# Three row transposes moved into the end of attention, the others moved behind the selection's spreading products, its scan and its ranks

## The chip, the cores and the metric

The kernel runs on one core of a Trainium2 chip. The metric is the device time of one execution in microseconds (us); the median of several executions is compared. The profile shows one execution, taken by the hardware profiler. Its engines are PE (TensorE matrix products; PEld are its weight loads), DVE (VectorE), ACT (ScalarE), POOL (GpSimd) and SP (which here only issues DMAs).

## The reference

Local attention with a few global keys, then a mixture of experts that keeps at most 80 tokens an expert:

```python
# attention: B=4, H=8, S=768, D=64; keep = 8 global keys, or the last 96 keys
scores = q @ k.T / sqrt(D) - slope[h] * dist          # masked where not kept
x = softmax(scores) @ v                               # 3072 rows of 512
# experts: E=8, F=1024
logits = x @ w_gate
expert_idx, gate_w = argmax(logits), max(softmax(logits))
for e in range(E):
    tok_idx = rows with expert_idx == e, the 80 with the largest gate_w
    out[tok_idx] = gate_w * (relu(x[tok_idx] @ w1[e]) @ w2[e])   # all other rows are 0
```

## The kernel before

The 3072 rows are 24 tiles of 128. The work has three parts one behind the other. **Attention** takes half a tile a step, 48 steps in all: scores, exponential, transposes, product with the values. Its result stays in SBUF turned: `uts[t]` holds tile t with the 512 features on the partitions. The gate's logits are computed on the way. The steps left at the end are written out by hand in the string `DRAIN`, one letter group for each call; the last idle products there are `busy(..., 4)`.

**Selection** (`slots`, `select`) finds the 80 best rows of each expert by a search in five rounds. A round's first product is the spreading product `jb` (L487): it hands a count of the round before (`gs`) to all partitions. DVE then rescales the keys (L489), takes a maximum (L495) and compares in three pieces (L502); PE counts the comparisons with 24 small products `cnt` (L507), and DVE compares the counts with the capacity (L511, `gs`). That is one chain between PE and DVE, each waiting for the other. The fifth round has no comparison: after L489 come two masks (L515, L516), a scan on DVE (L520), three products `rk` that turn the scan into ranks (L519, L522, L523), two DVE steps that make `slot` of them, four comparisons `at` (L556), 24 products `ix` (L560) and the reduction to row numbers `gi` (L563).

Beside this chain the 24 tiles are turned back and written to DRAM as rows, for the gathers: `rows(t, ...)` is four PE transposes into a PSUM tile `xp` (three buffers), one ACT copy (L97) into one of six places in SBUF (`room`, slot t % 6) and one DMA of 256 KB on SP's queue (L98). `slots` is a generator, and at each of its `yield`s `select` puts in `ROWS[i]` such tiles and `WARM[i]` idle products (`busy`, 480 columns, read by nobody). `SPLIT` says at which yield ACT rounds three weight pieces (`early`, L550). There are nine yields: after each round's maximum, after each round's `gs`, and after the ranks. All four compute engines run in the order in which the code is written. A copy into `room` waits until the DMA of the tile six before it has landed.

**Experts**: POOL gathers the rows of each expert from DRAM (L589), which needs `gi` and all 24 row DMAs; PE turns them (L621) and then computes the two layers (L627) without a pause to the end, while weights stream in.

PSUM has eight banks. Attention's pool `psa` uses seven, tags `sc` (two buffers of two banks), `tp0`, `tp1` and `u`. Selection opens its pools over the same banks.

Of the kernel before, what the change touches and what calls it, by code (L numbers as in the profile page):

```python
# [10 lines left out]
F32 = mybir.dt.float32  # L11
# [10 lines left out]
E, DM, DF = 8, 512, 1024  # L22
P = 128
NB = S // P
NT = B * NB
TURN = [*range(NT - NB), *range(NT - NB + 1, NT), NT - NB]
NP = H // 2
# [21 lines left out]

DRAIN = (  # L50
    "r a1 t45 w44 r r r n47 r r a2 t46 r r r r w45 r r r "
    "t47 w46 r b1 w47 r r b2 c1 c c2 c r r c3 r r c c r"
)
NORM = (("V", slice(2, 4)), ("G", slice(0, 2)))
ROWS = (4, 2, 5, 2, 4, 1, 3, 3, 0)
WARM = (0, 0, 0, 0, 1, 0, 0, 0, 9, 5)
SPLIT = (7, 8, 8)
FAR = 1.0e6
END = object()
SLOPES = [2.0 ** -(h + 1) for h in range(H)]  # L60
# [2 lines left out]
def fast_path(tc, a, out, cst, x_dram, inp):  # L63
    nc = tc.nc
# [3 lines left out]
    with ExitStack() as ctx:  # L68
# [20 lines left out]
                    in_=cst["zero"].unsqueeze(1).broadcast_to([P, 2, DM]),  # L89
                )  # L90

        def rows(t, pool, x):
            ut = uts.pop(t)
            xp = pool.tile([P, NP, P], F32, tag="xp", name=f"xp{t}")
            for pr in range(NP):
                T.transpose(out=xp[:, pr, :], in_=ut[:, pr, :], identity=ident)  # L96
            A.copy(out=x, in_=xp.rearrange("p q k -> p (q k)"))  # L97
            nc.sync.dma_start(out=x_dram[TURN[t] * P:(TURN[t] + 1) * P, :], in_=x)  # L98

        with tc.tile_pool(name="at_sb", bufs=2) as sp, tc.tile_pool(name="ps_a", bufs=1, space=PSUM) as psa, ExitStack() as pctx:  # L100
# [160 lines left out]
            def collect(t):  # L261
                g = next(i for i in range(len(GROUPS)) if t < sum(GROUPS[:i + 1]))
                n, t0 = GROUPS[g], sum(GROUPS[:g])
                if t == t0:
                    st["rt"] = Route(nc, sp, cst, t0, n)
                rt = st["rt"]
                if n < 3:
                    rt.one(lgs(t), t - t0)
                else:
                    lp = part(t).rearrange("p (q k) -> p k q", q=NP)  # L270
                    V.tensor_reduce(out=rt.lg[:, t - t0, :], in_=lp[:, :E, :], axis=AX.X, op=ALU.add)
                    if t == t0 + n - 1:
                        routing.append(rt.all())
                if t == t0 + n - 1:
                    if t < NT - 1:
                        routing.append(rt.rest(lps[:, 3 * P:3 * P + E], cst["capm"]))
# [5 lines left out]
            def go(g, n):  # L282
                for _ in islice(g, n):
                    pass

            def routes(n):
                for _ in range(n):
                    while routing and next(routing[0], END) is END:
                        routing.pop(0)
# [9 lines left out]
            for u in range(nu - 1):  # L299
# [47 lines left out]
                w44=lambda: weigh(u - 3), w45=lambda: weigh(u - 2), w46=lambda: weigh(u - 1), w47=lambda: weigh(u),  # L347
                n47=lambda: norm(u), a1=lambda: logits1(NT - 4, 2), a2=lambda: logits2(NT - 4, 2), b1=lambda: logits1(NT - 2, 1),
                b2=lambda: logits2(NT - 2, 1), c1=lambda: logits(NT - 1, (0, 1)), c2=lambda: logits(NT - 1, (2, 3)),
                c3=lambda: collect(NT - 1), r=lambda: routes(1), c=lambda: go(choice, 1),  # L350
            )
            for k in DRAIN.split():
                step[k]()
                if k == "b2":
                    rt = st["rt"]
                    choice, end = rt.choose(), rt.finish()
            scratch = psa.tile([P, 2, 512], F32, tag="sc", bufs=2, name="scratch")
            busy(nc, cst, scratch[:, 0], 4)
            go(choice, 99)
            routes(99)  # L360
            assert not routing
# [5 lines left out]

        hip = pool(name="hi", bufs=NHI[0], side="right")
        early = [hip.tile([P, DF], F32R, tag="hi", name=f"early{i}") for i in range(3)]
        room = inp.kt[1].rearrange("p q k -> p (q k)")[:, :6 * DM].rearrange("p (n d) -> p n d", n=6)  # L370
        select(tc, cst, lps, gs1, rows, raw, early, room)
        rctx.close()
        for _ in chain(wipe, ahead):
            pass
# [101 lines left out]
def slots(nc, sp, s2, pp, cst, gs, cap, slot):  # L476

    V, T, re, oh = nc.vector, nc.tensor, cst["re"], cst["oh"]
    k = P
    for i in range(5):
        n = 15 if i == 3 else 31
        jb = pp.tile([P, E], F32, tag="jb", name=f"jb{i}")
        T.matmul(jb, cst["ones32" if n > 15 else "ones16"][:k, :], gs[:k], start=True, stop=True)  # L487

        V.scalar_tensor_tensor(  # L489
            out=re, in0=re, scalar=512.0 if i == 0 else n + 1.0, in1=jb.unsqueeze(1).broadcast_to([P, NT, E]), op0=ALU.mult, op1=ALU.subtract,  # L490
        )
        if i == 4:
            break
        r = cst["left"][:, i % 2]
        V.tensor_reduce(out=r, in_=re, axis=AX.X, op=ALU.max)  # L495
        yield 1
        cm = s2.tile([P, NT, n], BF16, tag=f"cm{n}", name=f"cm{i}")
        cn = pp.tile([n, E], F32, tag="cnt", name=f"cnt{i}")
        t0 = 0
        for m in CUTS:  # L500
            tq = slice(t0, t0 + m)
            V.tensor_tensor(  # L502
                out=cm[:, tq, :], in0=r[:, tq].unsqueeze(2).broadcast_to([P, m, n]),
                in1=cst["kval"][:, :n].unsqueeze(1).broadcast_to([P, m, n]), op=ALU.is_ge,
            )
            for t in range(t0, t0 + m):
                T.matmul(cn, cm[:, t, :], oh[:, t, :], start=t == 0, stop=t == NT - 1)  # L507
            t0 += m
        k = n
        gs = s2.tile([k, E], BF16, tag=f"gs{n}", name=f"gs{i}")  # L510
        V.tensor_tensor(out=gs, in0=cn, in1=cap[:k], op=ALU.is_ge)  # L511
        yield 1
    mz = cst["mz"].rearrange("p (k t) -> p k t", k=2 * E)
    rev = re.rearrange("p t e -> p e t")
    V.tensor_scalar(out=mz[:, :E, 1:], in0=rev, scalar1=0.0, scalar2=None, op0=ALU.is_gt)  # L515
    V.tensor_scalar(out=mz[:, E:, 1:], in0=rev, scalar1=0.0, scalar2=None, op0=ALU.is_equal)  # L516
    cum = sp.tile([P, 2 * E, NT + 1], BF16, name="cum")
    rk = pp.tile([P, 2 * E, NT], F32, tag="rk", name="rk")
    T.matmul(rk, cst["tri"], mz[:, :, 1:], start=True, stop=False, skip_group_check=True)  # L519
    V.tensor_tensor_scan(  # L520
        out=cum.rearrange("p k t -> p (k t)"), data0=cst["keep"], data1=cst["mz"], initial=0.0, op0=ALU.mult, op1=ALU.add)
    T.matmul(rk[:, E:, :], cst["ones"], cum[:, :E, NT:NT + 1].broadcast_to([P, E, NT]), start=False, stop=False, skip_group_check=True)  # L522
    T.matmul(rk, cst["ones"], cum[:, :, :NT], start=False, stop=True, skip_group_check=True)  # L523
    yield 1
    wk = sp.tile([P, 2 * E, NT], F32, name="wk")
    V.tensor_tensor(out=wk, in0=rk, in1=mz[:, :, 1:], op=ALU.mult)
    with nc.allow_low_precision(reason="a sum of one integer and zeros; where slot is bfloat16, those up to 256 alone are asked for"):
        V.tensor_reduce(out=slot, in_=wk.rearrange("p k t -> p t k"), axis=AX.X, op=ALU.add)


def select(tc, cst, lps, gs1, rows, w, early, room):

    nc = tc.nc
    V, G, T = nc.vector, nc.gpsimd, nc.tensor
# [2 lines left out]
    with tc.tile_pool(name="sel2", bufs=2) as s2, tc.tile_pool(name="ps_s", bufs=1, space=PSUM) as pp, \  # L537
            tc.tile_pool(name="ps_r", bufs=3, space=PSUM) as pr, tc.manual_schedule(engines=ORDERED):
        slot = s2.tile([P, NT], BF16, name="slot", bufs=1)
        late = iter(range(NT))  # L540

        def more(n):
            for t in islice(late, n):
                rows(t, pr, room[:, t % 6])

        for i, _ in enumerate(slots(nc, s2, s2, pp, cst, gs1, cst["cap8"], slot)):
            more(ROWS[i])
# [605 lines left out]
```

## Time and profile before

| | |
|---|---|
| median of 3 runs | 287.97 us (286.52 to 288.28) |
| the profiled execution | 289.09 us, of which the span of its instructions is 287.4 us |
| PE busy in the span | 256.0 us (89%) |
| DVE, ACT, POOL busy | 215.0, 209.7, 123.2 us |
| bytes moved by DMA | 73.06 MB |

The profiled execution is 1.12 us above the median, and 1.7 us of it lie outside the span. Busy shares are means over the three parts, and the change touches the 30 us between 152 and 182 us of the span.

### The profile page before, as it was taken

How to read it: one execution, taken by the hardware profiler on the slowest of the kernel's cores; microseconds unless marked ns; L12 is line 12 of the kernel's file. 1: busy time of each engine (PE TensorE's matmuls, PEld its weight loads, DVE VectorE, ACT ScalarE, POOL GpSimd, SP SyncE). 2: the span in 40 equal slices, each digit the busy share in tenths (PEclk: the TensorE clock that was granted, in tenths of full speed). 3: DMA queues.
4: the chain of work that ended last, by engine and by line, in shares of the span. 5: the costliest groups of instructions: out<-in, count | busy, mean ns of one | idle time of the engine just before them, and what ended most of it. 6: DMA issues, size and time to landing. Idle time of an engine off the chain costs nothing. (4 is left out here: it accounts for less than half of the span.)

```text
span 287.4 us, 9517 instructions
## 1 busy us (share of the span) xinstructions
PE 256.0 (89%) x3538; PEld 187.0 (65%) x3538; DVE 215.0 (75%) x790; ACT 209.7 (73%) x596; POOL 123.2 (43%) x171
## 2 busy tenths in 40 slices
PE   2698799998988999999989997999999999999991
PEld 1486667676665777786757884466566666666660
DVE  4967567886657987689875346789998898988940
ACT  2778669976777968987863775378787978879730
POOL 5365554543553536553454000781506236063351
PEclk9999999999999999999996899799999999999998
DMA  6999999999999983541000794599999989990001
GB/s 180 326 339 378 291 368 323 316 339 320 349 379 392 383 269 115 141 137 42 2 5 20 294 381 187 148 294 348 395 386 395 397 320 401 336 375 16 25 15 41
DMA packets 37674, 73.06 MB, mean 254 GB/s; under 512 B 3284, under 2 KB 10324, under 8 KB 37620
## 3 DMA queue, kind: packets, MB, share of 16 engines
q1 hardware_dynamic: 36452, 69.74, 70.9%
q0 software_dynamic: 1024, 2.62, 3.0%
q8 instruction: 30, 0.49, 0.7%
q14 instruction: 24, 0.20, 0.2%
q10 hardware_dynamic: 144, 0.00, 0.0%
HBM read 58.46 MB, written 13.89 MB: 252 GB/s over the span
## 5 line engine op out<-in xcount | busy, mean ns | idle before, releaser
L145 ACT ACTIVATE pwz<-ts,nm 128x168 f32<-128x168 f32 (+1 forms) x192 | 80.1, 419 | 33.1 <-DVE nm L141 31.8
L158 POOL TENSOR_TENSOR pwz<-pwz,z 128x672 f32<-128x672 f32 (+2 forms) x48 | 60.2, 1253 | 71.4 <-ACT pwz L145 50.0
L141 DVE CUSTOM_DVE_ANT_0 ts<-sc,tab 128x168 f32<-128x168 f32 (+1 forms) x192 | 53.0, 314 | 27.0 <-PE sc L132 27.0
L132 PE MATMUL sc<-kt,q 64*64 64x104 f32 (+3 forms) x1088 | 44.4, 282 | 10.9 <-DVE kt L921 5.3
L608 POOL TENSOR_TENSOR w_3l<-w,w_3h 128x1024 fp32r<-128x1024 f32 x8 | 23.3, 2918 | 51.4 <-issue 34.6
L132 PEld LDWEIGHTS sc<-kt,q 64*64 64x64 f32 x1088 | 34.4, 141 | 14.4 <-issue 13.0
L145 ACT ACTIVATION_READ_ACCUMULATOR pwz<-ts,nm 128x1 f32 x192 | 36.0, 187 | 0.0
L203 PE MATMUL u<-ta,va 104*64 104x128 f32 (+1 forms) x384 | 32.5, 291 | 0.3 <-ACT kt L228 0.3
L174 PE MATMUL tp<-ident,pwz 64*128 64x64 f32 x384 | 22.9, 239 | 9.1 <-ACT ta L184 5.3
L608 DVE TENSOR_TENSOR w_0l<-w,w_0h 128x1024 fp32r<-128x1024 f32 x15 | 25.3, 1689 | 6.1 <-ACT w_0h L605 6.1
L174 PEld LDWEIGHTS tp<-ident,pwz 64*128 64x128 f32 x384 | 16.9, 142 | 17.3 <-POOL pwz L158 9.9
L213 PE MATMUL u<-ta,vb 64*64 64x64 f32 x640 | 27.3, 224 | 0.0
L213 PEld LDWEIGHTS u<-ta,vb 64*64 64x64 f32 x640 | 21.8, 134 | 6.9 <-issue 5.8
L185 DVE COPY ta<-tp 128x384 f32<-128x384 f32 (+1 forms) x48 | 25.4, 529 | 0.5 <-PE tp L174 0.3
L203 PEld LDWEIGHTS u<-ta,va 104*64 104x64 f32 (+1 forms) x384 | 20.6, 139 | 7.3 <-issue 3.1
L184 ACT COPY ta<-tp 128x384 f32<-128x384 f32 (+1 forms) x48 | 21.1, 440 | 1.4 <-PE tp L174 1.4
L608 DVE TENSOR_TENSOR w_2l<-w,w_2h 128x1024 fp32r<-128x1024 f32 x15 | 19.8, 1318 | 0.0
L97 ACT COPY kt<-xp 128x512 f32<-128x512 f32 x24 | 13.6, 589 | 6.9 <-PE xp L96 5.6
L608 DVE TENSOR_TENSOR w_1l<-w,w_1h 128x1024 fp32r<-128x1024 f32 x15 | 18.2, 1211 | 0.0
L605 ACT CAST w_2h<-w 128x1024 fp32r<-128x1024 f32 x15 | 15.9, 1057 | 1.2 <-PE hp L627 1.2
L605 ACT CAST w_3h<-w 128x1024 fp32r<-128x1024 f32 x16 | 16.7, 1044 | 0.0
L141 DVE DVE_READ_ACCUMULATOR2_ANT nm<- 128x1 f32 x192 | 15.8, 82 | 0.0
(391 smaller groups left out, 536.5 us busy)
## 6 DMA issues: line engine op xcount, KB each, us to landing
w<-in_w_dram SPq DMA_DIRECT2D x64, 512.0 KB
out_dram<-zero SPq DMA_DIRECT2D x12, 512.0 KB
x_dram<-kt SPq DMA_DIRECT2D x24, 256.0 KB
q<-in_q_dram SPq DMA_DIRECT2D x23, 256.0 KB
vb<-in_vb_dram SPq DMA_DIRECT2D x20, 256.0 KB
va<-in_va_dram SPq DMA_DIRECT2D x20, 208.0 KB
kt<-in_kT_dram SPq DMA_DIRECT2D x4, 816.0 KB
kt<-in_kT_dram SPq DMA_DIRECT2D x3, 544.0 KB
```

The costliest lines, as they stand in the source:

```text
L97: A.copy(out=x, in_=xp.rearrange("p q k -> p (q k)"))
L132: T.matmul(sc[64 * i:64 * i + 64, hh, pp, o:o + e - c], q[h, pr * P + 64 * i:pr * P + 64 * i + 64], kt[h, pr, c0 + c:c0 + e], start=True, ...
L141: V.tensor_tensor_reduce(out=ts[:, j, :w], in0=sc[:, hh, pp, :w], in1=cst["tab" if m else "tab0"][:, 2 * g + pp, hh, :], scale=-0.125, sca ...
L145: A.activation(out=pw[:, j, :w], in_=ts[:, j, :w], func=AF.Exp, bias=nm[:, j:j + 1], scale=-1.0, accum_out=z[:, j:j + 1],)
L158: eng.tensor_tensor(out=p, in0=p, in1=zs.unsqueeze(2).broadcast_to(list(p.shape)), op=ALU.mult)
L174: T.transpose(out=tps[i][:, 64 * j:64 * j + 64], in_=pw[hs[i], o:o + P], identity=ident[hs[i], hs[i]])
L184: A.copy(out=ta[:, 0, :n], in_=tps[0][:, :n])
L185: V.tensor_copy(out=ta[:, 1, :n], in_=tps[1][:, :n])
L203: T.matmul(up[64 * hh:64 * hh + 64, pr, :], va[:n, 64 * h:64 * h + 64], ta[:n, :, 64 * j:64 * j + 64], start=pp == 0 and (g == 0 or last), ...
L213: T.matmul(up[h, pr, 64 * i:64 * i + 64], vb[h, i, pr, :], ta[h, i, 256 + 64 * pp:320 + 64 * pp], start=False, stop=True, skip_group_check ...
L605: A.copy(out=hi, in_=src)
L608: eng.tensor_tensor(out=lo, in0=src, in1=hi, op=ALU.subtract)
```

## The change

`rows` is cut in two: `turned` issues the four transposes, `stored` the copy and the DMA. One iterator `due` hands the tiles out in order.

- In `DRAIN` the letters `x x x` turn tiles 0 to 2 ahead of `c3`, into PSUM tiles of attention's pool (tags `tp1`, `u`, `sc`), and `y y y` copy and store them behind `c3`. The four idle products go.
- In `slots` the yield after each `gs` goes; in its place are one in the fifth round behind L489 and one behind the scan. Seven yields are left: after each of the first four rounds' maximum, after the fifth round's L489, after the scan, after the ranks.
- `ROWS`, `WARM` and `SPLIT` become (4, 3, 3, 3, 2, 2, 4), three idle products after the ranks and five after `ix`, and the roundings of weights all behind the ranks.

```diff
 DRAIN = (
     "r a1 t45 w44 r r r n47 r r a2 t46 r r r r w45 r r r "
-    "t47 w46 r b1 w47 r r b2 c1 c c2 c r r c3 r r c c r"
+    "t47 w46 r b1 w47 r r b2 c1 c c2 c r r x x x c3 y y y r r c c r"
 )
-ROWS = (4, 2, 5, 2, 4, 1, 3, 3, 0)
-WARM = (0, 0, 0, 0, 1, 0, 0, 0, 9, 5)
-SPLIT = (7, 8, 8)
+ROWS = (4, 3, 3, 3, 2, 2, 4)
+WARM = (0, 0, 0, 0, 0, 0, 3, 5)
+SPLIT = (6, 6, 6)
...
-        def rows(t, pool, x):
+        room = inp.kt[1].rearrange("p q k -> p (q k)")[:, :6 * DM].rearrange("p (n d) -> p n d", n=6)
+        due = iter(range(NT))
+
+        def turned(t, xp):
             ut = uts.pop(t)
-            xp = pool.tile([P, NP, P], F32, tag="xp", name=f"xp{t}")
             for pr in range(NP):
-                T.transpose(out=xp[:, pr, :], in_=ut[:, pr, :], identity=ident)
-            A.copy(out=x, in_=xp.rearrange("p q k -> p (q k)"))
+                T.transpose(out=xp[:, pr * P:pr * P + P], in_=ut[:, pr, :], identity=ident)
+            return t, xp
+
+        def stored(t, xp):
+            x = room[:, t % 6]
+            A.copy(out=x, in_=xp)
             nc.sync.dma_start(out=x_dram[TURN[t] * P:(TURN[t] + 1) * P, :], in_=x)
...
-                c3=lambda: collect(NT - 1), r=lambda: routes(1), c=lambda: go(choice, 1),
+                c3=lambda: collect(NT - 1), x=lambda: edge.append(turned(next(due), spare.pop(0)())), y=lambda: stored(*edge.pop(0)), r=lambda: routes(1), c=lambda: go(choice, 1),
             )
+            edge = []
+            spare = [
+                lambda: psa.tile([P, 512], F32, tag="tp1", name="xp0"), lambda: psa.tile([P, 512], F32, tag="u", name="xp1"),
+                lambda: psa.tile([P, 2, 512], F32, tag="sc", bufs=2, name="xp2")[:, 0],
+            ]
...
-            scratch = psa.tile([P, 2, 512], F32, tag="sc", bufs=2, name="scratch")
-            busy(nc, cst, scratch[:, 0], 4)
...
@@ slots
         if i == 4:
+            yield 1
             break
...
         V.tensor_tensor(out=gs, in0=cn, in1=cap[:k], op=ALU.is_ge)
-        yield 1
...
     V.tensor_tensor_scan(
         out=cum.rearrange("p k t -> p (k t)"), data0=cst["keep"], data1=cst["mz"], initial=0.0, op0=ALU.mult, op1=ALU.add)
+    yield 1
...
@@ select
-            for t in islice(late, n):
-                rows(t, pr, room[:, t % 6])
+            for t in islice(due, n):
+                rows[1](*rows[0](t, pr.tile([P, DM], F32, tag="xp", name=f"xp{t}")))
```

The order of instructions on DVE, ACT, POOL and SP stays; only PE's changes. At the end of attention PE's rows stood so before (`lps<-oh,cf` are the counts of the last groups of tiles, `scratch` the idle products, `jb` the first spreading product):

```order
L473 LDWEIGHTS cf_3213
L473 MATMUL lps<-oh,cf_3213 127x8
L466 LDWEIGHTS ones
L466 MATMUL scratch<-svx,ones 128x480
L473 LDWEIGHTS cf_3260
L473 MATMUL lps<-oh,cf_3260 127x8
L487 LDWEIGHTS ones_75
L487 MATMUL jb_3329<-gs_82,ones_75 128x8
L96 MATMUL xp_3333<-ident,ut_379 128x128 x4
```

The two `ones`/`scratch` rows stand there four times; shown once. Now:

```order
L481 LDWEIGHTS cf_3213
L481 MATMUL lps<-oh,cf_3213 127x8
L98 MATMUL xp_3269<-ident,ut_379 128x128 x4
L98 MATMUL xp_3274<-ident,ut_379 128x128 x4
L98 MATMUL xp_3279<-ident,ut_630 128x128 x4
L481 LDWEIGHTS cf_3260
L481 MATMUL lps<-oh,cf_3260 127x8
L495 LDWEIGHTS ones_75
L495 MATMUL jb_3345<-gs_82,ones_75 128x8
```

Twelve transposes stand where four idle products stood. The `jb` behind them is the first instruction on a bank of selection's pools. In the built program it waits for ACT's last read of attention's PSUM: before, that was the exponential in `c3` (L397); now it is the third of the copies `y`.

From the fourth round to the fifth, PE's rows stood so before (the last `cnt` of the fourth round first):

```order
L507 MATMUL cnt_3587<-oh,cm_3586 15x8
L96 MATMUL xp_3617<-ident,kt_103 128x128 x4
L96 MATMUL xp_3624<-ident,kt_103 128x128 x4
L96 MATMUL xp_3631<-ident,kt_103 128x128 x4
L487 LDWEIGHTS ones_75
L487 MATMUL jb_3639<-gs_3637,ones_75 128x8
L519 LDWEIGHTS tri
L519 MATMUL rk<-mz,tri 128x384
L522 MATMUL rk<-cum,ones 128x192
L523 MATMUL rk<-cum,ones 128x384
L466 LDWEIGHTS ones
L466 MATMUL lps<-svx,ones 128x480
```

The last two stand there nine times. Now:

```order
L495 MATMUL jb_3576<-gs_3574,ones_75 128x8
L98 MATMUL xp_3579<-ident,ut_2403 128x128 x4
L98 MATMUL xp_3586<-ident,ut_2403 128x128 x4
L527 MATMUL rk<-mz,tri 128x384
L98 MATMUL xp_3599<-ident,kt_103 128x128 x4
L98 MATMUL xp_3606<-ident,kt_103 128x128 x4
L531 MATMUL rk<-cum,ones 128x192
L532 MATMUL rk<-cum,ones 128x384
L98 MATMUL xp_3615<-ident,kt_103 128x128 x4
L98 MATMUL xp_3622<-ident,kt_103 128x128 x4
L98 MATMUL xp_3629<-ident,kt_103 128x128 x4
L98 MATMUL xp_3636<-ident,kt_103 128x128 x4
```

The three tiles between the last `cnt` and `jb` are gone, and eight tiles now stand behind `jb`: two ahead of `rk`, two inside it and four behind, followed by three idle products. In the rounds before, nothing stands between `cnt` and the next `jb` any longer either.

## Rows read from the trace of the kernel before

**Rows 1.** The page: the span in 40 slices of 7.2 us, PE's granted clock in tenths of full speed, and GB/s moved.

```profile
PEclk9999999999999999999996899799999999999998
GB/s 180 326 339 378 291 368 323 316 339 320 349 379 392 383 269 115 141 137 42 2 5 20 294 381 187 148 294 348 395 386 395 397 320 401 336 375 16 25 15 41
```

**Rows 2.** Stretches of the span: start and end, length, then busy us (count) of PE, PEld, DVE, ACT and POOL, PE's granted clock (1.00 is 2.4 GHz, 0.50 is 1.2 GHz), DMA share and GB/s.

```profile
152.50:153.00 0.50, 0.49 (x6) 0.45 (x6) 0.32 (x3) 0.14 (x1) 0.00 (x0) 0.69 0.00 0
...
159.00:159.50 0.50, 0.50 (x19) 0.48 (x17) 0.00 (x0) 0.37 (x1) 0.00 (x0) 0.50 0.73 262
159.50:160.00 0.50, 0.50 (x5) 0.50 (x6) 0.15 (x1) 0.00 (x0) 0.00 (x0) 0.98 1.05 393
...
160.00:165.00 5.00, 5.00 (x60) 4.29 (x59) 1.98 (x7) 4.27 (x9) 0.00 (x0) 1.00 0.76 279
165.00:170.00 5.00, 5.00 (x64) 4.23 (x64) 3.26 (x11) 4.03 (x8) 0.00 (x0) 1.00 1.02 381
...
180.00:180.50 0.50, 0.50 (x3) 0.15 (x1) 0.41 (x4) 0.00 (x0) 0.00 (x0) 0.50 0.00 0
183.00:183.50 0.50, 0.50 (x3) 0.21 (x2) 0.50 (x1) 0.00 (x0) 0.24 (x1) 0.59 0.49 94
```

**Rows 3.** The timeline at the end of attention and in the first round: start us, length us, engine, line, operation, result <- operands, shape, count, and in brackets the idle time before it and what ended that.

```profile
152.60 0.44 PE L473 MATMUL lps<-oh,cf 128*127 128x8 bf16 x4
152.90 1.76 PE L466 MATMUL scratch<-svx,ones 128*128 128x480 bf16 x4
154.46 0.32 PE L473 MATMUL lps<-oh,cf 128*127 128x8 bf16 x2
154.81 0.17 DVE L364 TENSOR_TENSOR gs<-lps,capm 127x8 bf16<-127x8 f32 x1 [0.43 <-PE lps L473]
155.04 0.19 PE L487 MATMUL jb<-gs,ones 128*128 128x8 bf16 x1 [0.26 <-DVE gs L364]
155.09 3.66 PE L96 MATMUL xp<-ident,ut 128*128 128x128 f32 x16
156.22 0.59 ACT L97 COPY kt<-xp 128x512 f32<-128x512 f32 x1 [3.01 <-PE xp L96]
157.07 0.59 ACT L97 COPY kt<-xp 128x512 f32<-128x512 f32 x1 [0.27 <-PE xp L96]
158.68 0.80 PE L507 MATMUL cnt<-oh,cm 128*31 128x8 bf16 x24
```

**Rows 4.** The timeline of the second to the fifth round, the same columns.

```profile
160.14 3.23 ACT L97 COPY kt<-xp 128x512 f32<-128x512 f32 x6 [0.77 <-PE xp L96]
160.47 0.17 PE L487 MATMUL jb<-gs,ones 31*128 31x8 bf16 x1
160.57 2.52 PE L96 MATMUL xp<-ident,ut 128*128 128x128 f32 x20
161.46 1.07 DVE L502 TENSOR_TENSOR cm<-left,kval 128x279 bf16<-128x279 f32 x3
163.02 0.76 PE L507 MATMUL cnt<-oh,cm 128*31 128x8 bf16 x24
163.82 0.15 DVE L511 TENSOR_TENSOR gs<-cnt,cap 31x8 bf16<-31x8 f32 x1 [1.29 <-PE cnt L507]
164.74 0.17 PE L487 MATMUL jb<-gs,ones 31*128 31x8 bf16 x1
168.28 0.17 PE L487 MATMUL jb<-gs,ones 31*128 31x8 bf16 x1
168.39 1.53 PE L96 MATMUL xp<-ident,kt 128*128 128x128 f32 x12
169.27 0.67 DVE L502 TENSOR_TENSOR cm<-left,kval 128x135 bf16<-128x135 f32 x3
172.28 0.17 PE L487 MATMUL jb<-gs,ones 15*128 15x8 bf16 x1
```

**Rows 5.** The timeline from the last row copies and the fifth round's masks to the first expert, the same columns.

```profile
171.05 2.63 ACT L97 COPY kt<-xp 128x512 f32<-128x512 f32 x4 [0.20 <-PE xp L96]
173.51 0.33 PE L519 MATMUL rk<-mz,tri 128*128 128x384 bf16 x1 [1.05 <-DVE mz L516]
174.53 0.24 PE L522 MATMUL rk<-cum,ones 128*128 128x192 bf16 x1 [0.70 <-DVE cum L520]
177.17 2.85 PE L560 MATMUL ix<-bx,at 128*80 128x48 bf16 x24 [0.40 <-DVE at L556]
180.06 0.17 DVE L563 TENSOR_REDUCE gi<-ix 80x8 int32<-80x16 f32 x1 [1.99 <-PE ix L560]
180.53 1.21 POOL L589 DMA_INDIRECT q<-x_dram,gi  x1 [22.38 <-DVE xsel L565]
183.97 0.44 PE L621 MATMUL xf<-ident,q 80*128 80x80 f32 x4
```

**Rows 6.** POOL's queue ahead of the first gather (its four waits for the row DMAs: count, duration ns min/median/max, first and last start us), and two stretches of the span, columns as in rows 2.

```profile
L589 POOLq EVENT_SEMAPHORE  x4: 43/43/629, 175.3 to 177.2; - x4
175.50:176.00 0.50, 0.50 (x5) 0.20 (x3) 0.47 (x2) 0.50 (x2) 0.00 (x0) 1.00 0.76 287
176.00:176.50 0.50, 0.50 (x4) 0.19 (x2) 0.50 (x1) 0.50 (x1) 0.00 (x0) 1.00 0.12 45
```

**Rows 7.** The experts, in stretches of 20 us, columns as in rows 2.

```profile
185.00:205.00 20.00, 20.00 (x103) 13.26 (x104) 19.16 (x21) 17.12 (x23) 10.16 (x7) 1.00 1.03 331
```

More of the change, by code (lines that the diff above doesn't have):

```diff
@@ L369, in fast_path @@
         early = [hip.tile([P, DF], F32R, tag="hi", name=f"early{i}") for i in range(3)]
-        room = inp.kt[1].rearrange("p q k -> p (q k)")[:, :6 * DM].rearrange("p (n d) -> p n d", n=6)
-        select(tc, cst, lps, gs1, rows, raw, early, room)
+        select(tc, cst, lps, gs1, (turned, stored), due, raw, early)
         rctx.close()
@@ L528, in slots, with select @@
         V.tensor_reduce(out=slot, in_=wk.rearrange("p k t -> p t k"), axis=AX.X, op=ALU.add)
-def select(tc, cst, lps, gs1, rows, w, early, room):
+def select(tc, cst, lps, gs1, rows, due, w, early):
     nc = tc.nc
@@ L539, in select @@
         slot = s2.tile([P, NT], BF16, name="slot", bufs=1)
-        late = iter(range(NT))
         def more(n):
-            for t in islice(late, n):
-                rows(t, pr, room[:, t % 6])
+            for t in islice(due, n):
+                rows[1](*rows[0](t, pr.tile([P, DM], F32, tag="xp", name=f"xp{t}")))
         for i, _ in enumerate(slots(nc, s2, s2, pp, cst, gs1, cst["cap8"], slot)):
```

## The prediction

> **What bounds the kernel now.** I read the page's slices first: PE's clock dips and the bytes moved change between slices 21 and 25 alone [rows 1], which is the selection. Then the experts by stretches: PE is busy 20.00 of 20 us at the full clock [rows 7], so that part is a block of PE work that starts when the first gather's rows are turned, and moves one to one with it. What remains is the road from the end of attention to the first gather at 180.53 [rows 5]. I read its timeline by the starts of `jb`, since each round begins there: 155.04, 160.47, 164.74, 168.28 and 172.28 [rows 3, 4]. The rounds last 5.43, 4.27, 3.54 and 4.00 us, and from the fifth `jb` to the gather it is 8.25 us. DVE's own steps take little of a round: from `jb` to the end of its comparisons 160.47 to 162.53, 2.06 us (in the fourth round, with 15 columns for 31, 168.28 to 169.94, 1.66). The rest is PE: DVE waits 1.29 us for the counts in the second round, and `jb` comes 0.77 us after the end of `gs` in the third (163.97 to 164.74) because turned rows stand between [rows 4].
>
> The clock matters too. It fell to half at about 152.7 and rose at 159.5, fell at 180.0 and rose at about 183.4 [rows 2]. At half, a tile of four transposes takes 0.855 us (ACT's copies start 156.22, 157.07 [rows 3]); at the full clock twelve take 1.53 us, some 0.46 us a tile [rows 4].
>
> **The change, part by part.** All is summed against the profiled execution, 289.09 us, which is 1.12 above the median.
>
> *The start.* Four idle products go, twelve transposes come. The idle products began at 152.90 [rows 3], at the half clock, and so will the transposes, since nothing ahead of them changes. Their third copy on ACT begins where the third copy of the first round began after its transposes: 1.13 us for the first and 0.855 for each further, 2.84 us [rows 3], so at 155.7, and ends 0.59 later, at 156.3. The counting products behind the transposes are free at about 155.5 and `gs` at 156.0, but `jb` now waits for that third copy: a wait that the change adds. Behind it on PE stand the first round's tiles, and DVE waits for it. `jb` goes from 155.04 to 156.35: **+1.3 us**. (At the full clock the copies alone would pace it, three at 0.54 a copy [rows 4] from 153.6, and `jb` would come at about 155.3, +0.3.)
>
> *The first round.* Four tiles as before. If the clock stays at half until 159.5, as before, 14 or 15 of the 16 transposes run cold (0.214 us each from 156.4), the counts start at 159.75, take 0.80 [rows 3], and with `gs` the next `jb` comes at 160.75. The round lasts 4.4 for 5.43 us, **-1.0**: it begins later but ends beside the rise, and the two tiles between its counts and the next `jb` are gone. If the clock rises one step earlier, the tiles cost 1.8 us, the fourth waiting for a buffer, and the round lasts about 2.85 us, -2.6.
>
> *The rounds two to four.* Three tiles stand behind each `jb`: 1.53 us from 0.11 behind it [rows 4], over before DVE's comparisons end at 2.06. What is late next is DVE: the last five counts follow its last comparison, at 0.03 us each (24 in 0.76 [rows 4]). I put them and two handovers at 0.38, `gs` at 0.15 and the step to `jb` at 0.06 (154.98 to 155.04 [rows 3]): 2.65 us a round. In the fourth round the counts follow the tiles instead, 1.5 + 0.76 + 0.03 + 0.21, 2.5 us. No round shows counts that wait for DVE alone; the bounds are 0.3 and the 0.69 us from 169.94 to the next `gs` in the fourth round (counts from 169.85, ended 170.6 [rows 4] reads as this), so 2.5 to 3.0 a round. Together 7.8 for 11.81 us, **-4.0**. ACT's copies need 3 x 0.54 a round and stay hidden.
>
> *The ranks.* From the fifth `jb`: two tiles are turned by 1.05 us, before the masks end at 1.2 (`rk` at 173.51, 1.23 behind [rows 5]), hidden. Two more behind the first `rk` end at 2.33, where the scan is over at 2.25 [rows 5]: +0.1. Then four tiles at ACT's pace end at 4.6, three idle products at 5.2, and `ix` could have begun at 5.0 (4.9 before, 177.17 [rows 5]): +0.15. So `gi` comes 0.25 us later behind its `jb`. But the last copy now ends at 5.7 behind `jb`, not at 1.4 (173.68 [rows 5]). Before, the last DMA followed that copy, its traffic ended at about 176.0, and POOL's last wait opened at 177.2 + 0.63 = 177.8, 2.7 us before the gather [rows 6]: 1.8 us from the end of traffic to the landing. Now the last eight tiles are copied every 0.55 us or so, the DMA engines need 0.67 a tile (256 KB at 385 GB/s [rows 2]), so traffic ends at about 7.4 behind `jb`, the rows have landed at 9.2, and the gather starts at 9.4 instead of 8.25: **+1.15 us**, of which 0.25 is the chain and 0.9 a wait that was hidden. Its ends: 8.5 if a landing with short queues costs nothing more than the chain, and 9.9 if it takes the 4.1 us of 173.7 to 177.8 again.
>
> *The rest.* The gather's rows reach PE at 183.97, 3.4 us behind it [rows 5]; the idle products between move earlier with `ix` and stay within that. The rounding of weights on ACT now begins at 5.7 behind `jb` and ends at 8.7; its first taker on DVE comes after `gi`, at 9.2. Both cost nothing; with that cover gone it would be some tenths. The copies' six places in SBUF are taken again after six tiles, about 5 us in these rounds, against some 3.2 us from copy to landing with short queues (0.75 + 0.65 + 1.8, from the first DMA's start to the last landing): no wait to speak of.
>
> *Sum*: 1.3 - 1.0 - 4.0 + 1.15 = -2.55 us. 289.09 becomes 286.5; against the median, 287.97 becomes **285.4**.
>
> **A rule that speaks against it.** From 160 to 170 us PE ran row transposes, counts of eight columns and one idle product, and its clock was granted at 1.00; it rose at 159.5 after 4.4 us in which PE had done 16 transposes and the counts [rows 2, 3]. So by the rows transposes raise and hold the clock. The Trainium skill ("TensorE: Matmul & The Clock Gate", Part 4: PE-mode transpose) says that the full clock does not engage for transposes, which do not count as busy in the same way. By that rule this trace should have stayed at half through the selection; it did not, so the rows decide, and the rule keeps a small chance below.
>
> **The rivals.**
>
> *The clock rises earlier (20 in 100).* Twelve transposes and the next round's follow each other more closely than before, with one gap for the third copy. If they raise the clock by about 156.1 the first round is the short one: another -1.6, -4.15 in all, **283.8**. For it: the rise at 159.5 came behind just such work [rows 2, 3]. Against: before, the idle products and four transposes from 152.9 on did not raise it. The same end is reached if the fall comes later in most executions than in the profiled one.
>
> *The gain is lost again at the experts (17 in 100).* The idle products behind `ix` end earlier against the rows' landing, which is late now; PE then stands idle for 1 to 2 us ahead of L621, and the clock, which fell at 180.0 behind the light `ix` products [rows 2], may be at half when the dense products start. Before, idle products bridged this until 183.97. Up to 3 us of product at half speed cost 1.5: -1.05, **286.9**. For it: the fall at 180.0; against: `ix` now has seven tiles and three products right ahead of it, where PE idled before.
>
> *Transposes do not hold the clock (8 in 100), slower.* At half, three tiles cost 2.57 us, more than DVE's 2.06, and each round becomes 0.1 + 2.57 + 0.76 + 0.24 = 3.67 us: the fifth `jb` comes at 156.35 + 4.5 + 11.0 = 171.85, only 0.4 earlier. Behind it the tiles lie in the chain: `rk` waits 0.6, the ranks 1.6 more, and four tiles and three products (3.42 + 1.2 us) end near 9.0, so `ix` starts there for 4.9 and the gather at 12.3 behind `jb`. 184.2 for 180.53: +3.6, **291.6**. It decides if the clock reads 0.50 beyond the first round. Against it stands the 1.00 from 160 to 170 [rows 2]; for it, that a round now holds three tiles where the second held five, and no idle product until the ranks.
>
> **How the numbers follow.** The forecast has 55 in 100. Its own range: rounds at 3.0 and the landing at 9.9 give up 1.4 of the gain (286.8), rounds at 2.5 and the gather at 8.5 add 1.2 (284.2). With the rivals that hold most of the rest, 283.5 to 287.8 leaves out the slow case and the ends beyond. A measurement of this kernel tells a change of about 1% (2.9 us) from none. The forecast lies 0.3 us short of that, so two in five of its chance count as faster; with the earlier clock that makes 0.43 faster, 0.47 within 1%, 0.10 slower.
>
> **What would show it.** Right: `jb` starts 2.5 to 3.0 us apart in rounds two to four; DVE's wait for the counts falls from 1.29 to about 0.4; the first `jb` follows the third copy on ACT; POOL's last wait for the row DMAs opens after `gi`, so the gather is released by the rows and not by DVE; PE busy 20.00 in 20 us in the experts. Wrong: `jb` with the first `gs` and not with the copy; a granted clock of 0.50 in rounds two to five or at the first dense products; `ix` released by the tiles ahead of it; a gather that starts right behind `gi`.

## The result and the profile after

The changed kernel took 290.91 us in the median (288.01 to 293.61) against 288.56 (286.52 to 294.58) for the kernel before on the same chip: 1.0066 times as long, 95% interval 1.004 to 1.0093. That is some 1.9 us more where the forecast had 2.55 us less, and above the predicted range. Executions of one kernel come in a faster and a slower state, and every ratio here compares the faster ones alone, so it differs from that of the medians. The profiled execution took 290.35 us, its span is 288.6 us. In the kernel after, the lines named so far stand about eight further down: `jb` is L495, the row copies L103, `ix` L568, `gi` L571, the gathers L597, the weights' roundings and subtractions L613 and L616, the turning of gathered rows L629, the dense products L635.

First the page, in 40 slices of 7.2 us, as [rows 1]:

```profile
PEclk9999999999999999999997999589999999999997
GB/s 176 320 309 391 288 361 320 332 335 329 365 367 391 385 266 124 189 76 40 2 5 160 315 332 171 207 347 235 343 303 399 348 371 390 315 387 51 23 7 51
```

The dip at the end of attention is smaller than before; a new and deeper one stands in the slices at 180 and 187 us, where the first dense products lie. Then the timeline of the end of attention and of the five rounds (columns as in [rows 3]):

```profile
152.09 2.80 PE L98 MATMUL xp<-ident,ut 128*128 128x128 f32 x12
154.93 0.59 ACT L103 COPY kt<-xp 128x512 f32<-128x512 f32 x1 [0.27 <-PE xp L98]
155.57 0.17 PE L495 MATMUL jb<-gs,ones 128*128 128x8 bf16 x1 [0.56 <-ACT kt L103]
...
158.54 0.16 PE L495 MATMUL jb<-gs,ones 31*128 31x8 bf16 x1 [0.24 <-DVE gs L520]
...
160.99 0.15 DVE L520 TENSOR_TENSOR gs<-cnt,cap 31x8 bf16<-31x8 f32 x1 [0.40 <-PE cnt L516]
161.19 0.16 PE L495 MATMUL jb<-gs,ones 31*128 31x8 bf16 x1 [0.24 <-DVE gs L520]
...
163.84 0.16 PE L495 MATMUL jb<-gs,ones 31*128 31x8 bf16 x1 [0.24 <-DVE gs L520]
...
166.38 0.16 PE L495 MATMUL jb<-gs,ones 15*128 15x8 bf16 x1 [0.24 <-DVE gs L520]
```

The rounds last 2.97, 2.65, 2.65 and 2.54 us for the 5.43, 4.27, 3.54 and 4.00 us of before [rows 3, 4], and DVE waits 0.40 us for the counts instead of 1.29. The fifth `jb` starts 5.90 us earlier. Of this 0.82 us are not the change's: in this execution attention ended so much sooner (the counts ahead of the transposes start at 151.78, before at 152.60 [rows 3]). All of the gain and more is lost behind it, as the timeline from `ix` to the end of the first twelve dense products shows:

```profile
171.32 2.81 PE L568 MATMUL ix<-bx,at 128*80 128x48 bf16 x24
...
173.98 2.59 PE L474 MATMUL lps<-svx,ones 128*128 128x480 bf16 x12
174.17 0.17 DVE L571 TENSOR_REDUCE gi<-ix 80x8 int32<-80x16 f32 x1 [1.98 <-PE ix L568]
175.30 1.23 DVE L616 TENSOR_TENSOR w_0l<-w,early 128x1024 fp32r<-128x1024 f32 x1
176.44 1.22 DVE L616 TENSOR_TENSOR w_1l<-w,early 128x1024 fp32r<-128x1024 f32 x1
176.55 12.97 SPq L83 DMA_DIRECT2D w<-in_w_dram  x6
177.05 1.70 POOL L597 DMA_INDIRECT q<-x_dram,gi  x1 [18.75 <-DVE w_0l L616]
182.68 0.77 PE L629 MATMUL xf<-ident,q 80*128 80x80 f32 x4 [6.12 <-DMA q<-x_dram,gi]
183.96 0.72 PE L635 MATMUL hp<-early,xt0h 128*80 128x512 f32 x1 [0.52 <-ACT xt0h L622]
...
189.17 0.55 PE L629 MATMUL xf<-ident,kt 80*128 80x80 f32 x4
```

`gi` is 5.89 us earlier than before, the gather only 3.48 us (180.53 [rows 5]), the rows at PE 1.29 us, the first dense product 0.97 us. And then twelve dense products take 5.21 us (183.96 to 189.17, where the next rows are turned) for 2.91 us before (184.93 to 187.84). From the trace of before, with the first load of weights:

```profile
182.44 4.53 SPq L83 DMA_DIRECT2D w<-in_w_dram  x3
...
184.93 0.46 PE L627 MATMUL hp<-early,xt0h 128*80 128x512 f32 x1 [0.52 <-ACT xt0h L614]
...
187.84 0.44 PE L621 MATMUL xf<-ident,kt 80*128 80x80 f32 x4
```

The stretches (columns as in [rows 2]) say at which clock, and what the DMA engines did meanwhile:

```profile
155.00:155.50 0.50, 0.01 (x1) 0.10 (x1) 0.42 (x3) 0.50 (x1) 0.38 (x3) 0.74 0.83 299
...
156.00:161.00 5.00, 4.71 (x76) 4.15 (x74) 3.56 (x13) 3.62 (x7) 1.89 (x8) 1.00 0.81 297
161.00:166.00 5.00, 4.56 (x74) 4.01 (x73) 3.45 (x12) 2.95 (x6) 0.00 (x0) 1.00 0.82 302
...
174.00:174.50 0.50, 0.50 (x5) 0.27 (x5) 0.29 (x3) 0.50 (x1) 0.00 (x0) 1.00 0.87 328
174.50:175.00 0.50, 0.50 (x5) 0.21 (x3) 0.47 (x4) 0.26 (x1) 0.00 (x0) 1.00 0.07 25
...
179.00:179.50 0.50, 0.00 (x0) 0.00 (x0) 0.00 (x0) 0.00 (x0) 0.45 (x1) 0.66 0.99 365
...
184.00:189.00 5.00, 5.00 (x12) 3.03 (x13) 4.91 (x5) 2.85 (x3) 3.96 (x3) 0.50 0.69 208
189.00:189.50 0.50, 0.50 (x5) 0.33 (x4) 0.15 (x1) 0.00 (x0) 0.00 (x0) 0.60 1.13 299
...
183.96:203.96 20.00, 20.00 (x93) 13.16 (x94) 17.12 (x18) 15.12 (x21) 6.36 (x4) 0.86 0.85 273
```

PE finished its idle products at 176.57, stood idle for 6.12 us, and its clock fell to half in the middle of that; it rose again only at about 189.4. In 20 us from the first dense product 93 instructions start for the 103 of [rows 7]. POOL's waits for the row stores, as [rows 6]:

```profile
L597 POOLq EVENT_SEMAPHORE  x4: 43/43/622, 173.6 to 175.5; - x4
```

The last one ends at 176.1, 1.9 us behind `gi`, and the gather follows 0.9 us later. So the stores' landing starts the gather now, as forecast; the bracket behind the gather names a subtraction on DVE, which a run below rules out. What the forecast did not see stands in the line above the gather: the loads of the experts' weights (512 KB each), which are released by DVE's first subtraction, 2.4 us behind `gi`, now start 0.5 us *ahead* of it. Before they started 1.9 us behind it (182.44).

**The account**, profile against profile: the fifth `jb` -5.90; from there to the gather 10.67 for 8.25, +2.42; from the gather to the first dense product 6.91 for 4.40, +2.51; the first twelve dense products at half clock 5.21 for 2.91, +2.30. Sum +1.33; the spans differ by 1.2. Without the 0.82 us by which attention ended sooner it would be about +2, near the 1.9 of the ratio.

### The profile page after: what moved, and what is told of

Its sections match the earlier page's. It is cut to its first block, busy times and chain, and to the rows that moved or that the text cites. A ratio compares the mean times of both kernels' runs of the same rounds, so it can differ in the third digit from the quotient of the medians.

```text
span 288.6 us, 9495 instructions
## 1 busy us (share of the span) xinstructions
PE 252.5 (87%) x3527; PEld 187.0 (65%) x3527; DVE 219.9 (76%) x790; ACT 209.1 (72%) x596; POOL 129.8 (45%) x171
## 5 line engine op out<-in xcount | busy, mean ns | idle before, releaser
L138 PE MATMUL sc<-kt,q 64*64 64x64 f32 (+3 forms) x1088 | 44.2, 281 | 10.8 <-DVE kt L929 5.4
L616 POOL TENSOR_TENSOR w_3l<-w,w_3h 128x1024 fp32r<-128x1024 f32 x8 | 30.0, 3749 | 50.1 <-issue 30.2
L616 DVE TENSOR_TENSOR w_0l<-w,w_0h 128x1024 fp32r<-128x1024 f32 x15 | 31.2, 2079 | 2.4 <-ACT w_0h L613 2.2
L616 DVE TENSOR_TENSOR w_2l<-w,w_2h 128x1024 fp32r<-128x1024 f32 x15 | 18.1, 1210 | 0.5 <-ACT w_2h L613 0.5
L616 DVE TENSOR_TENSOR w_1l<-w,w_1h 128x1024 fp32r<-128x1024 f32 x15 | 18.2, 1211 | 0.1
L103 ACT COPY kt<-xp 128x512 f32<-128x512 f32 x24 | 12.8, 592 | 6.7 <-PE xp L98 4.2
L613 ACT CAST w_2h<-w 128x1024 fp32r<-128x1024 f32 x15 | 15.9, 1057 | 1.2 <-PE hp L635 1.2
L613 ACT CAST w_3h<-w 128x1024 fp32r<-128x1024 f32 x16 | 16.7, 1043 | 0.0
L613 ACT CAST w_1h<-w 128x1024 fp32r<-128x1024 f32 x15 | 15.7, 1047 | 1.0 <-PE hp L635 1.0
```

Source lines behind the costliest of these rows:

```text
L103: A.copy(out=x, in_=xp)
L138: T.matmul(sc[64 * i:64 * i + 64, hh, pp, o:o + e - c], q[h, pr * P + 64 * i:pr * P + 64 * i + 64], kt[h, pr, c0 + c:c0 + e], start=True, ...
L613: A.copy(out=hi, in_=src)
L616: eng.tensor_tensor(out=lo, in0=src, in1=hi, op=ALU.subtract)
```

## The experiments

The theory (T) from these traces: two losses that feed each other eat the gain. The gathered rows queue behind weights, and the idle PE lets its clock fall. Rivals: DVE's subtractions hold up POOL's gather (P); the rows are slow because they are read right behind the stores, whatever the weights do (S); the transposes at the end of attention cost the time (D). The traces read below are of executions that lie up to 4.1 us from their kernel's median, so the ratios (95% intervals in brackets) give the verdicts and the traces only what happened inside.

**More idle products**, to keep PE going until the rows arrive:

```diff
-            busy(nc, cst, lps, 7)
+            busy(nc, cst, lps, 34)
             tokens(0)
```

> The changed kernel with 34 for 7 idle products ahead of the first expert's rows; PE has nothing else to do there until the rows land (176.6 to 182.65 us in the changed kernel's trace). Theory T (the rows land late because weight loads run ahead of them, and PE, idle until then, starts the dense products at half clock): the rows still land at about 182.6, but the granted clock is 1.00 when the dense products start, which gives back the half-clock time, 2.6 us: ratio to before about 0.997. Rival C (the half clock there comes from somewhere else, not from the idle time): clock 0.50 at the dense products as before, no gain, ratio 1.006.

Measured: 0.9998 (0.9953 to 1.0043). The clock stayed at 1.00 and the loss against before is gone, though the rows are as late as in the kernel after (5.6 us behind the gather). Its timeline, and 20 us from the first dense product:

```profile
175.90 1.75 POOL L597 DMA_INDIRECT q<-x_dram,gi  x1 [18.30 <-DVE w_0l L616]
181.50 0.47 PE L629 MATMUL xf<-ident,q 80*128 80x80 f32 x4 [0.56 <-DMA q<-x_dram,gi]
182.48 0.46 PE L635 MATMUL hp<-early,xt0h 128*80 128x512 f32 x1 [0.51 <-ACT xt0h L622]
...
182.48:202.48 20.00, 20.00 (x103) 13.31 (x104) 19.15 (x21) 17.08 (x23) 9.07 (x6) 1.00 0.91 315
```

**Rows ahead of the weights, first try.** A DMA of 32 bytes on SP's queue that reads the gathered rows, to hold the loads behind it:

```diff
                 gather(e)
+            nc.sync.dma_start(out=held[0, 0:1, 0:8], in_=xgs[0][:1, :8])
             prepare(2)
```

> The changed kernel with the weight loads held on SP's queue until the first expert's gathered rows have landed (a DMA of 32 bytes that reads those rows stands ahead of them). Theory T: the rows land some 3.2 us after the gather is issued, as before the change, instead of 5.6; PE's first turn of rows comes about 2.3 us earlier than in the changed kernel, and idle time and half clock shrink with it: ratio to before 0.99 to 1.00. Rival S (the rows are slow because they are read right behind the stores, whatever the weights do): still 5 us or more from gather to rows, ratio 1.006 or above.

Measured: 1.0075 (1.0026 to 1.0123). As a test of the order it failed: the DMA came behind two loads on SP's queue, not ahead of all. What it does tell: those two, 1 MB, are enough.

```profile
176.65 1.53 SPq L83 DMA_DIRECT2D w<-in_w_dram  x2
177.03 1.82 POOL L597 DMA_INDIRECT q<-x_dram,gi  x1 [18.22 <-DVE w_0l L616]
182.76 0.77 PE L629 MATMUL xf<-ident,q 80*128 80x80 f32 x4 [6.09 <-DMA q<-x_dram,gi]
```

**Rows ahead of the weights.** Now the DMA is the first on SP's queue, and goes into the tile of the first weight, so that all loads come behind it:

```diff
+                if hold:
+                    nc.sync.dma_start(out=t[:1, :8], in_=hold.pop()[:1, :8])
                 yield nc.sync.dma_start(out=t.rearrange("p (c f) -> p c f", c=k), in_=src[:, k * c:k * c + k])
...
                 gather(e)
+            hold.append(xgs[0])
             prepare(2)
```

> The changed kernel with all weight loads of the experts held behind the landing of the first gathered rows: a DMA of 32 bytes from those rows to the first weight tile now stands first on SP's queue (in e2_rows_first it stood behind two loads of 512 KB). Theory T: the first gather is still issued about 0.5 us behind the end of the first weight subtraction on DVE, but its rows land 3.2 to 3.8 us behind it instead of 5.5, so PE turns them about 2 us earlier than in the changed kernel: ratio 0.996 to 1.003. Rival S (reading right behind the stores is slow): 5 us or more, ratio 1.005 or above. Rival P (DVE's two subtractions, which run while POOL makes up the gather, slow it, and the loads do not matter): 5 us or more as well.

Measured: 1.0012 (0.9967 to 1.0057). With no weights beside them the rows come 3.86 us behind the gather, right behind the same stores, so S falls. The gather itself is no earlier against `gi` (171.87, 2.8 us). PE still idles 2.57 us ahead of the rows, and the clock falls to half at about 178.8:

```profile
174.66 1.78 POOL L600 DMA_INDIRECT q<-x_dram,gi  x1 [18.25 <-DVE w_0l L619]
178.52 0.48 PE L632 MATMUL xf<-ident,q 80*128 80x80 f32 x4 [2.57 <-DMA q<-x_dram,gi]
179.32 5.75 SPq L86 DMA_DIRECT2D w<-in_w_dram  x6
...
179.51:199.51 20.00, 20.00 (x98) 13.27 (x99) 18.25 (x21) 15.98 (x22) 9.61 (x7) 0.93 0.98 323
```

**DVE's subtractions behind the first take of rows**:

```diff
-            prepare(2)
             busy(nc, cst, lps, 7)
             tokens(0)
-            prepare(2)
+            prepare(4)
```

> The changed kernel with the first two weight subtractions on DVE (and the loads that they set free) behind the first expert's rows instead of ahead of them. Rival P: the gather is issued within 0.3 us of POOL's last wait for the stores instead of 0.9, and takes 1.0 to 1.2 us instead of 1.7. Theory T: its rows land 3.2 us behind it. Together PE turns rows about 3 us earlier than in the changed kernel; the second dense product then waits about 1.5 us for the first subtraction: ratio to before 0.992 to 1.001. Rival S: rows 5 us behind the gather.

Measured: 1.0055 (1.0005 to 1.0104). With `gi` at 173.65 the gather comes 2.85 us behind it, as in the kernel after (2.88), so the subtractions do not delay it, and the bracket now names the stores (`x_dram`); they lengthen its own work, which takes 1.21 us here for 1.70. P falls as the cause of the start and stays for half a microsecond. The rows reach PE 3.44 us behind the gather, but the gain is lost again: PE idles 3.90 us ahead of them, the clock is at half from 178.9 to 185.7, and the second dense product waits 0.94 us for the subtraction.

```profile
176.50 1.21 POOL L597 DMA_INDIRECT q<-x_dram,gi  x1 [18.72 <-DMA x_dram<-kt]
179.94 0.77 PE L629 MATMUL xf<-ident,q 80*128 80x80 f32 x4 [3.90 <-DMA q<-x_dram,gi]
...
181.61 1.21 DVE L616 TENSOR_TENSOR w_0l<-w,early 128x1024 fp32r<-128x1024 f32 x1
```

**Both mends at once**: the held weights, and 16 idle products for 7.

> The kernel after with both mends of the earlier runs: the loads of the experts' weights held behind the landed rows, and 16 idle products for 7 ahead of the first take of the rows. Selection and row stores are as in the kernel after, so the gather still starts about 2.8 us behind gi, waiting for the stores. Theory T (two losses, rows that queue behind the weights' loads and dense products at half clock): rows reach PE 3.2 to 3.9 us behind the gather, the clock is 1.00 at the first dense products, these take 0.40 us each, and the time falls by another 1 us or so against the held kernel alone: ratio 0.990 to 0.999, near 286.5 us. Rival W (holding the weights costs as much as it gives, since the first expert's products wait for them): PE waits for weights of the first expert by 1 us or more behind the first dense product, and the ratio stays at 1.000 or above although the clock is 1.00.

Measured: 0.9946 (0.9907 to 0.9985). This is the pair to read beside the kernel after: `gi` at 174.21 and the gather at 177.09 are the same to 0.04 us, so all that differs lies behind.

```profile
177.09 1.70 POOL L600 DMA_INDIRECT q<-x_dram,gi  x1 [18.35 <-DVE w_0l L619]
180.92 0.47 PE L632 MATMUL xf<-ident,q 80*128 80x80 f32 x4 [2.49 <-DMA q<-x_dram,gi]
181.73 4.42 SPq L86 DMA_DIRECT2D w<-in_w_dram  x5
181.91 0.46 PE L638 MATMUL hp<-early,xt0h 128*80 128x512 f32 x1 [0.52 <-ACT xt0h L625]
...
181.90:201.90 20.00, 20.00 (x103) 13.30 (x104) 19.14 (x21) 17.09 (x23) 10.16 (x7) 1.00 0.98 326
```

The first dense product is 2.05 us earlier, and the span 284.2 for 288.6 us; the other 2.35 us are nearly all the twelve first products, which no longer run at half clock and take 2.92 us for 5.21. One thing stays open: PE idles 2.49 us here ahead of the rows, about as long as with the rows held alone, yet the clock stays at 1.00. A wait of this length cost the clock in one trace and not in the other, so its length alone does not decide it; the clock before it differed too (with the rows held alone it stood at 0.50 from 172.0 to 175.4, here at 1.00). Against the kernel after, the two mends gave 0.5% (rows held) and 0.7% (idle) alone and 1.2% together. These are differences of ratios, each uncertain by about 0.5%. W falls: PE has no wait for a weight there.

**Rows stored earlier**: four tiles a round, none behind the ranks, where idle products take their place.

```diff
-ROWS = (4, 3, 3, 3, 2, 2, 4)
-WARM = (0, 0, 0, 0, 0, 0, 3, 5)
+ROWS = (4, 4, 4, 3, 3, 3, 0)
+WARM = (0, 0, 0, 0, 0, 0, 9, 5)
```

> The changed kernel with four tiles in the first three rounds, three in the fourth, three behind the fifth's spreading product, three behind the scan and none behind the ranks (idle products there, nine). The last row stores then are issued about 3 us earlier. Theory T: they have landed when the row numbers are known, so the gather starts 0.3 us behind those, ahead of the weight loads, the rows come 3.3 us later and PE's gap is short enough for the full clock: dense products start near 179, 5 to 6 us before those of the kernel before: ratio 0.980 to 0.988. Rival S: gather earlier, but its rows still 5 us or more behind it: ratio 0.99 to 1.00. A rival that the rounds become longer with four tiles: rounds of 3.2 us or more for 2.65, ratio 0.99 or above.

Measured: 0.9894 (0.9825 to 0.9962). The stores have landed before `gi`, the gather starts right behind it and the weights behind the gather, without any hold:

```profile
176.74 0.17 DVE L571 TENSOR_REDUCE gi<-ix 80x8 int32<-80x16 f32 x1 [1.98 <-PE ix L568]
177.21 1.21 POOL L597 DMA_INDIRECT q<-x_dram,gi  x1 [19.44 <-DVE xsel L573]
179.12 6.71 SPq L83 DMA_DIRECT2D w<-in_w_dram  x5
180.61 0.47 PE L629 MATMUL xf<-ident,q 80*128 80x80 f32 x4 [1.47 <-DMA q<-x_dram,gi]
181.59 0.46 PE L635 MATMUL hp<-early,xt0h 128*80 128x512 f32 x1 [0.52 <-ACT xt0h L622]
...
181.59:201.59 20.00, 20.00 (x96) 13.07 (x97) 17.88 (x20) 15.86 (x21) 8.46 (x7) 0.91 1.03 339
```

The ratio falls short of the 0.980 to 0.988 that were expected. A round with four tiles lasts about 3.0 us instead of 2.65, and `gi` comes 8.46 us behind the fifth `jb` for 7.79. It pays all the same: from the first `jb` to the first dense product 26.55 us with its first round at half clock, for 28.39 in the kernel after and 29.89 before. PE idles only 1.47 us ahead of the rows, and still the clock falls, at 182.5.

**The same with 16 idle products for 7**:

> e3_rows_early with 16 for 7 idle products ahead of the first expert's rows, which fill the 1.5 us in which PE was idle there. Theory T: the clock stays at 1.00 into the dense products, which in e3_rows_early fell to half for 3 us from 182.5: 1.5 us faster than e3_rows_early, ratio to before 0.982 to 0.988. Rival C: no difference to e3_rows_early (0.989).

Measured: 0.9892 (0.9815 to 0.997), median 285.32 against 286.38 without the extra products. Its trace has the shortest road, 25.08 us from the first `jb` (154.50), and the full clock behind it:

```profile
179.58 0.46 PE L635 MATMUL hp<-early,xt0h 128*80 128x512 f32 x1 [0.51 <-ACT xt0h L622]
...
179.58:199.58 20.00, 20.00 (x103) 13.32 (x104) 19.18 (x21) 17.14 (x23) 10.17 (x7) 1.00 1.03 333
```

Its ratio is the same as without them, so what the idle products add here is not settled. Both versions beat the kernel before by their intervals, with six executions each; which of the two is the faster is not shown.

**The change in halves.** First the selection alone: attention's end as before, the three tiles turned in later rounds.

```diff
-    "t47 w46 r b1 w47 r r b2 c1 c c2 c r r x x x c3 y y y r r c c r"
+    "t47 w46 r b1 w47 r r b2 c1 c c2 c r r c3 r r c c r"
...
+            scratch = psa.tile([P, 2, 512], F32, tag="sc", bufs=2, name="scratch")
+            busy(nc, cst, scratch[:, 0], 4)
             go(choice, 99)
-ROWS = (4, 3, 3, 3, 2, 2, 4)
+ROWS = (4, 4, 4, 4, 2, 2, 4)
```

> The changed kernel's selection alone: the end of attention has its four idle products again, no tiles there, and the rounds take four tiles each. Rival D (the transposes at the end of attention and the wait for their copies cost the time): 1 us or more faster than the changed kernel, ratio 0.997 to 1.002. Theory T: the first spreading product comes about 0.8 us sooner after the last counts than in the changed kernel, but the first stores leave later and the gather waits for the last one all the same, the weight loads run ahead, and the dense products start at half clock: ratio 1.003 to 1.010.

Measured: 1.0064 (1.0018 to 1.011), the loss of the whole change. This alone does not clear the start, since the rounds hold four tiles here: in its trace it is 12.16 us from the first `jb` to the fifth, for 10.81 in the kernel after.

Then the three tiles at the end of attention alone, with the yields and `SPLIT` of before:

```diff
-ROWS = (4, 3, 3, 3, 2, 2, 4)
-WARM = (0, 0, 0, 0, 0, 0, 3, 5)
+ROWS = (3, 2, 4, 2, 4, 1, 3, 2, 0)
+WARM = (0, 0, 0, 0, 1, 0, 0, 0, 9, 5)
```

> The other half alone: tiles 0 to 2 at the end of attention as in the changed kernel, but the selection's yields, idle products and roundings as before, with 21 tiles put in (3, 2, 4, 2, 4, 1, 3, 2, 0). Theory T: the first spreading product comes some 0.3 to 1.3 us later behind the counts, the rounds lose about as much, since three tiles fewer stand between; the stores end before the row numbers are known and the gather runs ahead of the weights: ratio to before 0.994 to 1.003. Rival D (the transposes at the end of attention cost the time): 1.004 or more.

Measured: 0.994 (0.9885 to 0.9995). No row is turned behind the ranks here, and with the transposes at the end of attention the kernel is faster than before, where D asked for 1.004 or more. D falls.

**Control**: the kernel before with 16 idle products for 7.

> Control: the kernel before with 16 idle products for 7 ahead of the first take of the rows and nothing else. Theory T: there the rows come 3.4 us behind the gather and the dense products start at the full clock, so the idle products cover a wait that costs nothing: ratio 0.997 to 1.003, the gather right behind gi, rows at PE 3.4 us behind it. Rival I (the idle products help this program whatever the selection does, and the gain of the earlier runs with more of them has nothing to do with the change): ratio 0.995 or below, with a clock at the first dense products that is higher than in the kernel before.

Measured: 1.0006 (0.9961 to 1.0051). No gain shows, so rival I falls: before the change there was no wait for these products to bridge. The control is not quite free of a cost of its own. In its one trace, of an execution 2.5 us above the median, the products ran on to 186.70, 5.26 us behind the gather at 181.44, so the rows were turned some 1.8 us later than the 3.4 us expected.

## Why the prediction was wrong

**The rounds held.** Rounds two to four were put at 2.65, 2.65 and 2.5 us and last 2.65, 2.65 and 2.54: DVE is the bound, with the counts 0.4 us behind it. So `jb` to `jb` needs no more than that as long as three tiles stand behind it; four make it 3.0.

**The start held; the first round went better, by the clock.** `jb` does wait for the third copy, and that copy starts 2.84 us behind the first transpose, to the hundredth as worked out. From the counts ahead of the transposes to `jb` it is 3.79 us (151.78 to 155.57) for 2.44 before (152.60 to 155.04), +1.35 where +1.3 was forecast. That `jb` came at 155.57 and not at 156.35 is attention, which ended 0.82 us sooner in this execution. The clock rose at 155.3, not at 159.5, which is the first rival: the round lasts 2.97 us. The rise came behind twelve transposes and two counts. How long the clock stays at half here is not a property of the code: in the traces of five variants with the same code up to there it did not fall at all, and from the counts to `jb` it was 2.5 us, so that the start cost next to nothing; with the rows stored earlier it rose only at 158.6, and the first round took 4.62 us, near the forecast 4.4. What decides it is open.

**The ranks: right mechanism, wrong size.** 9.4 us from the fifth `jb` to the gather were forecast, 9.9 as the upper end; it was 10.67. The chain itself cost nothing: `gi` came 7.79 us behind the fifth `jb`, before 7.78, where 0.25 us more were forecast. All of the 2.4 us is wait. Against the 9.4 us that were forecast, three terms differ: the traffic ended 8.1 us behind `jb` for 7.4; from there to the end of POOL's last wait it took 1.6 us for 1.8; and from that wait to the gather 0.9 us for 0.2. The last was a step hidden before, when the waits had ended 2.7 us ahead of the gather; what it consists of no run shows.

**The rest: the step that failed.** "The gather's rows reach PE ... 3.4 us behind it" was carried over from [rows 5], and the experts were taken to shift one to one with it. The 3.4 us held only because the weights' loads started behind the gather, and nothing in the program orders them so. Both hang on `gi`: the loads by six small steps of DVE and a subtraction, 2.4 us, the gather by 0.47 us. When the gather was made to wait for the stores instead, 2.9 us behind `gi`, the loads passed it. The rows then took 5.6 us, of which 1.8 go when the loads are held back and another 0.4 when the subtraction isn't beside the gather. Nor did the experts shift one to one: from the first dense product to the end of the span it is 104.6 us, before 102.5; with the clock kept at 1.00, as with more idle products, it is 102.1.

**The second rival came true, and dearer.** It priced an idle PE of 1 to 2 us and up to 3 us of products at half speed, 1.5 us. PE idled 6.1 us, and 5.2 us of products ran at half speed, 2.3 us. Its sum (286.9) lacked the 2.5 us more from the gather to the first dense product: 2.2 us by which the rows came late, and 0.3 us for turning them at half clock. It also took over the ranks' term, which was 1.27 us too small.

With both losses taken away the change does pay: 0.9946, 0.4 to 2.7 us by the interval. The forecast's -2.55 us with the gather 1.27 us and the rows 0.39 us later than forecast leave -0.9; with a first `jb` and a first round that are better by 0.8 and 1.4 us, as in that trace too (155.60, and 2.98 us), -3.1, against spans that differ by 3.2 (284.2 for 287.4). That it fits so well is in part luck: the counts at the end of attention, which the change does not touch, start 2.4 us apart in two of these traces (150.79 with the rows held, 153.18 in the first try). And what the selection's half adds is not shown: the end of attention alone gave 0.994 too. Only the versions with the rows stored earlier lie lower, and their intervals overlap with these.

## What to carry to other kernels

When a step gets a new, later last wait, list what else is released by its old one and shares its way: here the weights' loads overtook the gather, and a latency read from the trace of before no longer held. A wait ahead of a long block of matrix products costs the wait and can cost the clock behind it, so price both, and look at the granted clock of the first products. Work moved off one chain has to land before the next consumer asks: some 0.4 us more in each of two rounds and 0.7 us behind the fifth `jb` were cheaper here than four tiles at the end.

## What the runs showed of the hardware

**A gather that starts beside a subtraction on DVE.** Its work on POOL took 1.21 us with DVE free and 1.70 to 1.82 us when it started within the second subtraction; there it ended 1.08 to 1.09 us behind the subtraction's end in five runs (178.75 against 177.66 in the kernel after). A subtraction that began 0.65 us behind the gather's start cost nothing (181.18 in the kernel before, whose gather took 1.21 us [rows 5]). The Trainium skill ("SBUF — State Buffer", SBUF: two separate sides, the box on DVE blocking DMA) says that POOL is locked out of the port pair that it shares with DVE, and cannot write the descriptors of its DMAs, while DVE runs an operation in a two-port performance mode; the box names an fp32 copy, not a subtraction of two operands as here. That a gather which starts within a subtraction ends at a fixed time behind it fits that; the second case, where the two overlap by 0.56 us and neither is longer, does not follow from it.

**Transposes and the clock.** From 156 to 167.6 us of the kernel after PE ran nothing but row transposes, counts of eight columns and `jb`, no idle product, and was granted 1.00 throughout (the stretches of 156 to 166 us above), as in [rows 2]. So the slow rival falls, and what the Trainium skill ("TensorE: Matmul & The Clock Gate", Part 4: PE-mode transpose) says, as the prediction tells it, does not hold for this kernel.
